# First 512 tokens as one block, blocks of 384 and 512 in turn, and the second batch's masks on VectorE

## The chip, the cores and the metric

The kernel runs on one core of one Trainium2 chip. The core has a matrix engine (TensorE, PE in the rows; PEld are its weight loads), a vector engine (VectorE, DVE), a scalar engine for activation functions (ScalarE, ACT), GpSimd (POOL) and SyncE (SP), which here issues all DMAs. The metric is the device time of one execution in microseconds.

## The reference, cut to what matters

Attention over 4 batches, 8 heads, 576 tokens and 64 dimensions a head; heads 0 to 3 see the 32 tokens before them (local), heads 4 to 7 see the tokens at a distance that is a multiple of 32 (strided). Its result goes through two feed-forward layers of 2304 tokens, width 512 and inner width 2048:

```python
scores = scale * q @ k.T                       # per batch and head
scores = where(mask_local or mask_strided, scores, -1e9)
x = softmax(scores) @ v                        # -> 2304 x 512
h = x @ moe_w_in ;  g = h * tanh(softplus(h)) ;  x = g @ moe_w_out
h = x @ moe2_w_in ; g = h - tanh(h)            ; y = g @ moe2_w_out
```

## The kernel before, in words

All products are done as three fp32r matmuls on high and low parts (high by high, low by high, high by low), which is why each weight and each activation is split into two parts.

**Attention** is done in half-pairs: a pair is two heads of one batch (`pair`, L492), each of its two halves 8 (strided) or 6 (local) score tiles. For a half PE computes the scores into two PSUM tiles `sps` (`score`, L577), VectorE takes the row maxima, ScalarE the exponentials `p`, PE transposes them (`ptps`, L697), they are copied to SBUF (`pT`), and PE multiplies with v (`ops`, L715). A batch in `LEAN` (L489) gets its mask from PE: before the scores, one bf16 matmul with the identity adds the mask to each of the two PSUM tiles (L586), VectorE then takes one maximum over a whole tile (`row_max`, L617), and the exponentials read PSUM. A batch that is not lean has no mask matmul; VectorE adds the mask and takes the maximum tile by tile in one instruction each (`masked_max`, L622) and writes the masked scores to SBUF. In a lean batch the division by the sum may be put on ScalarE (L665) or VectorE; in others it is VectorE's alone (L688). Batch 0 (`BY_PE`) has its sums made by PE (`tot`, L731).

**The first layer** goes over blocks of tokens, `blocks[0] = [256, 256, 512, 384, 512, 384]` (L262). A step is one block and one of 16 chunks c of the inner width (`step`, L841): 12 matmuls into `h` (L855), Mish on ScalarE into `B` (L874), the split of B into `gh` and `gl`, and two steps later (`LAG`) 12 matmuls into the four accumulators `acc` (L906). The moving operand is as wide as the block, so a matmul has 256, 384 or 512 columns. The first two blocks share the weights' arrival: five steps of block 0 run first, then block 1 and block 0 take turns (L349 to L351), and both write halves of the same accumulators. In batch 0, the second halves of the two local pairs (`LATE`, L462) have late due times, since block 0 needs only the first 256 tokens.

**The weights** of the first layer come by DMA as pairs of 32-bit words and are made into fp32 on VectorE (L414, L419, L424, three passes of 512 columns) and split (`wi`, `wo`, L449 to L455), while the first two blocks run. The second layer (`unit`, L1228) goes over its own blocks and is not touched, but for which spare buffers hold its parts of x.

**The order of all work** is set by `Plan.run` (L131): it lists tasks with due times and costs, and writes each engine's instructions in the order in which its own calculation has them start. Where it has PE idle for over 0.12 us before 196.6 us (`FILL`), it puts small filler matmuls there (`fill`, L475 to L479), at most the first part of the program. Batch b's attention is spread over the time before the block that needs it (L373 to L378); block data for the later blocks are stored to HBM and loaded again (`x_load`, L811), then split into `xh` and `xl` (`x_split`, L793).

Of the kernel before, what the change touches and what calls it, by code (L numbers as in the profile page):

```python
# [217 lines left out]
def pe_cost(n):  # L218
    return {256: 0.12, 384: 0.174, 512: 0.227}.get(n, 0.0004375 * n + 0.007)
# [23 lines left out]
def attention_two_moe(  # L243
# [15 lines left out]
    NC = 16  # L259
    WIN = 32  # L260
    scale = 1.0 / float(D) ** 0.5
    blocks = [[256, 256, 512, 384, 512, 384], [512] * 4 + [256]]  # L262
    TB = (512, 384)
    LAG = 2

# [9 lines left out]
    }  # L275
    starts = [[sum(bl[:j]) for j in range(len(bl))] for bl in blocks]

    pieces2 = [(0, starts[0][2])] + list(zip(starts[0], blocks[0]))[2:]
    x2d = {
        (p, i): dram.tile([128, n], F32, name=f"x2d{p}_{i}")  # L280
        for p in range(KC)
# [64 lines left out]
    add = plan.add  # L346


    steps = [(0, 0, c) for c in range(HEAD)]  # L349
    for c in range(NC):  # L350
        steps += [(0, 1, c)] + ([(0, 0, c + HEAD)] if c + HEAD < NC else [])  # L351
    steps += [(0, j, c) for j in range(2, len(blocks[0])) for c in range(NC)]
    NU, HALF = NC // 2, 256
    steps += [(1, j, u) for j in range(len(blocks[1])) for u in range(NU)]
    step_of = {x: s for s, x in enumerate(steps)}
# [2 lines left out]
    for l, j, c in steps:  # L358
        if l == 0 and j == 0:
            t_ = max(t_, FIRST + PACE * c)  # L360
        due.append(t_)
        if l == 0:
            t_ += 24 * pe_cost(blocks[l][j]) + (ATTEND if 1 < j < 5 else 0.0)
        else:
            t_ += (42 if blocks[1][j] > HALF else 24) * pe_cost(HALF) + 6 * blocks[1][j] // 128 * pe_cost(DM)
    due += [t_, t_ + 4, t_ + 8, t_ + 12]
    first_use = [min(step_of[0, j, c] for j in range(2)) for c in range(NC)]


    def block_of(token):  # L370
# [2 lines left out]
    x_due = [FIRST] + [due[step_of[0, block_of(S * b), 0]] - XLEAD for b in range(1, B)]  # L373
    ATT = {}
    for b in range(1, B):
        since = max(x_due[b - 1], due[step_of[0, 1, 0]])
        gap = (x_due[b] - since) / KC
        ATT[b] = (x_due[b] - KC * gap, gap)  # L378

# [79 lines left out]


    pairs = [(b, p) for b in range(B) for p in (2, 3, 0, 1)]
    LATE = (2, 3)  # L462
    pass
    AT = ["at0", "at1"]
    EARLY = ["h0", "h1", "acc0", "acc1", "acc2", "acc3"]

# [19 lines left out]
    last_s, last_load = {}, {}  # L486


    BY_PE, LEAN = (0,), (0, 1)  # L489
    ON_ACT = [(0, 0), (0, 1), (1, 0), (1, 1)]  # L490

    def pair(i):  # L492
# [272 lines left out]

        last_pv = []

        inner = starts[0][2]
        x_slot = ["xr0", "wi9", "wo9", "wi8"][i] if first else "xr0"
        xb = Buf([x_slot], 5) if first else Buf([x_slot], 1)  # L770
        done = [half_pair(0), half_pair(1)]
        plan.link(*done)
        cols = slice(inner, S) if first else slice(0, S)
        if first:
            for j in range(2):
                t0, n = starts[0][j], blocks[0][j]
                x_split(0, j, p, [done[0]] if i in LATE and j == 0 else done,
                        lambda t0=t0, n=n: st["x"][:, t0:t0 + n], xb,
                        k0 + 3 if j == 0 else due[step_of[0, 1, 0]] - 3)
            free_first[x_slot] = [split[j][p][1] for j in range(2)]  # L780
            for n, what in enumerate("qkv"):
                free_first[slot_of_first(i, what)] = last_s[i] if what != "v" else last_pv
        x_store[p, b] = add({SP: 0.45}, lambda e: nc.sync.dma_start(out=xd[p, b][:, cols], in_=st["x"][:, cols]),
                            k0 + 4, done, give=[xb], dma=0.3 if first else 0.9)
# [26 lines left out]
    def x_load(l, j, p, key):  # L811
        n, t0 = blocks[l][j], starts[l][j]
        if l == 0:
            pieces = [(b, b * S, b * S + S) for b in range(B)]
        else:
            pieces = [(i, s, s + m) for i, (s, m) in enumerate(pieces2)]
        cut = []
        for i, a, e in pieces:
            lo, hi = max(a, t0), min(e, t0 + n)
            if lo < hi:  # L820
                cut.append((i, lo, hi, a))
        buf = Buf(TMP, 2)
# [8 lines left out]
        after = [x_store[p, c[0]] if l == 0 else x2_store[p, 0, c[0] + 1] for c in cut]  # L831
        J = len(blocks[0]) * l + j
        x = add({SP: 0.45 * len(cut)}, load, key - 5, after + [last_g1[J - 2]], take=[buf], dma=0.7)
        x_split(l, j, p, [x], lambda: h["t"], buf, key)


# [4 lines left out]
    def step(s):  # L841
# [48 lines left out]
        B_done[s] = lo  # L890

        m = KC

        both = J < 2
        wide = starts[0][2] if both else n
        cols = slice(starts[0][J], starts[0][J] + n) if both else slice(0, wide)
        opens, closes = c == 0 and J != 1, c == NC - 1 and J != 0
        k2 = due[s + LAG] + 0.1
        for f in range(m):
            def gemm2(e, f=f):  # L900
                w = wts[l, "o", c]
# [14 lines left out]
            if closes:  # L916
                eb = Buf(TMP, 1)

                def evac(e, f=f, eb=eb):
                    t_ev[J, f] = t = sb([128, wide], F32, eb.slot, "ev")  # L920
                    if e == ACT:
                        nc.scalar.activation(out=t, in_=acc[f], func=ACTF.Copy, scale=2.0 ** -8)
                    else:
                        nc.vector.tensor_single_scalar(out=t, in_=acc[f], scalar=2.0 ** -8, op=ALU.mult)

                def store(e, f=f):
                    nc.sync.dma_start(out=x2d[f, j - 1], in_=t_ev[J, f])
# [192 lines left out]
    def factors(j, key, ready):  # L1120
# [5 lines left out]
        def load_of(x):  # L1126

            lower, half = x
            a0 = t0 + HALF * half
            cut = []  # L1130
            for i, (a, m) in enumerate(pieces2):
                lo, hi = max(a, a0), min(a + m, a0 + HALF)
                if lo < hi:
                    cut.append((i, lo, hi, a))
            buf = Buf(TMP, 2 if x == X22 else 1)

            def load(e):
# [5 lines left out]
            after = [x2_store[2 * lower + k, 0, i[0] + 1] for k in range(2) for i in cut] + old  # L1143
            return add({SP: 0.9 * len(cut)}, load, key - 5 + len(raw_loads), after, take=[buf], dma=0.7), buf

        def tiles():
# [9 lines left out]
            if J % 2 == 0:  # L1156
                lo = [hi.pop()] + [one_(sb([128, 2, HALF], F32R, slot, "xq")) for slot in ("q0", "q1", "k0", "k1")]
                t = sb([128, 4, HALF], F32R, "v", "xq")
                lo += [one_(t[:, :2]), one_(t[:, 2:])]
            else:  # L1160
                hi += [one_(sb([128, 2, HALF], F32R, "xr0", "xq"))]
                t = sb([128, 9, HALF], F32R, "pp", "xq")
                lo = [one_(t[:, 2 * i:2 * i + 2]) for i in range(4)]
                lo += [one_(cols(W2[u, 3][:, 1, :])) for u in (2 * NS, 2 * NS + 1)]
                lo += [two_(*(sb([128, 1, HALF], F32R, f"pT{i}", "xq") for i in range(2)))]
            xq[J] = list(zip(hi, lo))
            return xq[J]

# [246 lines left out]
    with tc.manual_schedule():  # L1415
# [8 lines left out]
        for c in range(NC):  # L1424
            for half in "io":
# [10 lines left out]
        for s in range(2 * NC):  # L1436
            step(s)
        last = len(blocks[0]) - 1
        for J in range(2, last + 1):
            if J < 2 + B - 1:  # L1440
                for i in range(KC * (J - 1), KC * J):
                    pair(i)
            for p in range(KC):
                x_load(0, J, p, due[NC * J] - XSPLIT + 0.7 * p)
# [33 lines left out]
        x, y = LATE  # L1478
        order[2 * x:2 * x + 4] = [(x, 0), (y, 0), (x, 1), (y, 1)]
# [57 lines left out]
```

## Time and profile before

| | |
|---|---|
| median of 3 runs | 892.72 us (891.67 to 892.78) |
| profiled execution | 891.31 us, span of the instructions 889.5 us |
| PE busy | 882.3 us (99% of the span) |
| VectorE busy | 593.0 us (67%) |
| ScalarE busy | 429.3 us (48%) |
| granted TensorE clock | 0.999 |

A row of the timeline is: start in us, length in us, engine, line, operation, out<-in, partitions by columns, count; a bracket at the end is idle time before it and what ended it. Matmul ends are modelled, so the spacing of starts is the better measure of what one costs. A program's time is some 1.8 us over its span.

### The profile page before, as it was taken

What the parts mean: (1) busy time and instruction counts of PE and PEld (TensorE: products, weight loads), DVE (VectorE), ACT (ScalarE), POOL (GpSimd) and SP (SyncE); (2) the same over time, 40 slices, a digit from 0 to 9 for tenths busy, and PEclk for the clock granted to TensorE, in tenths of its full rate; (3) what the DMA queues carried; (4) which work ended last, traced back from release to release, by engine and by line L of the source; (5) the groups of instructions that cost most, each with busy time, mean ns of one, the idle gap of its engine ahead of it and who ended that gap; (6) DMA issues with size and microseconds to landing.
All of it is one profiled execution on the core that took longest, in us unless ns stands there. A gap on an engine that the chain in (4) does not pass through costs nothing.

```text
span 889.5 us, 16480 instructions
## 1 busy us (share of the span) xinstructions
PE 882.3 (99%) x6080; PEld 788.3 (89%) x6080; DVE 593.0 (67%) x1578; ACT 429.3 (48%) x910; POOL 2.4 (0%) x13
## 2 busy tenths in 40 slices
PE   8999999999999999999999999999999999999998
PEld 7899999877778999888999999898999889998896
DVE  6999998556565657778776885575457545555533
ACT  7999999656446625443444532252224222322211
POOL 1000000000000000000000000000000000000000
PEclk9999999999999999999999999999999999999999
DMA  9981113411112149877787443352235223655531
GB/s 308 379 340 55 59 59 102 150 62 33 63 66 91 43 149 317 253 260 258 252 282 233 133 152 102 112 190 95 96 132 176 95 96 119 209 169 162 175 125 62
DMA packets 84657, 138.19 MB, mean 155 GB/s; under 512 B 10016, under 2 KB 37152, under 8 KB 84576
## 3 DMA queue, kind: packets, MB, share of 16 engines
q1 hardware_dynamic: 84576, 137.14, 46.1%
q8 instruction: 48, 0.79, 0.4%
q14 instruction: 33, 0.27, 0.1%
HBM read 107.22 MB, written 29.88 MB: 154 GB/s over the span
## 4 chain that ended last, share of the span: by engine, by line
PE 93%; ACT 4%; DVE 1%; DMA 1%; issue 0%; SPq 0%; ACTq 0%
PE acc L1382 22%; PE h L855 22%; PE acc L906 22%; PE hx L1245 18%; PE hx L1262 3%; PE sps L589 2%; PE ops L715 2%; PE ptps L697 2%; ACT p L645 1%; DMA kT<-in_k_dram 1%; ACT stwo L402 0%; ACT pT L449 0%; ACT L193 0%; ACT stwi L402 0%; ACT dd L735 0%
## 5 line engine op out<-in xcount | busy, mean ns | idle before, releaser
L855 PE MATMUL h<-xh,wi 128*128 128x256 f32 (+2 forms) x768 | 215.1, 342 | 0.6 <-ACT B L874 0.5
L906 PE MATMUL acc<-gh,wo 128*128 128x256 f32 (+2 forms) x768 | 196.5, 341 | 0.0
L1382 PE MATMUL acc<-w,gh 128*128 128x512 f32 x576 | 179.1, 392 | 0.0
L1245 PE MATMUL hx<-xq,w 128*128 128x256 f32 x1280 | 174.1, 284 | 0.0
L1245 PEld LDWEIGHTS hx<-xq,w 128*128 128x128 f32 x1280 | 167.6, 191 | 6.5
L855 PEld LDWEIGHTS h<-xh,wi 128*128 128x128 f32 x768 | 137.9, 189 | 14.4 <-ACT B L874 1.0
L906 PEld LDWEIGHTS acc<-gh,wo 128*128 128x128 f32 x768 | 132.1, 189 | 10.4
L855 PE MATMUL h<-xl,wi 128*128 128x256 f32 (+2 forms) x384 | 129.4, 337 | 0.1
L906 PE MATMUL acc<-gl,wo 128*128 128x256 f32 (+2 forms) x384 | 128.9, 336 | 0.0
L1382 PEld LDWEIGHTS acc<-w,gh 128*128 128x128 f32 x576 | 103.2, 188 | 18.1 <-DVE gh L451 0.4
L1382 PE MATMUL acc<-w,gl 128*128 128x512 f32 x288 | 112.2, 389 | 0.0
L1333 ACT ACTIVATE th<-hx 128x256 f32<-128x256 f32 x48 | 18.5, 385 | 160.2 <-PE hx L1245 120.1
L193 ACT ACT_TABLE_LOAD x70 | 89.8, 1283 | 1.2
L874 ACT ACTIVATE B<-h 128x256 f32<-128x256 f32 (+2 forms) x96 | 46.9, 492 | 89.5 <-PE h L855 87.0
L1338 DVE SCALAR_TENSOR_TENSOR H<-hx,th 128x256 f32<-128x256 f32 x48 | 20.3, 423 | 98.7 <-ACT th L1333 98.6
L455 DVE TENSOR_TENSOR gl<-B,gh 128x256 fp32r<-128x256 f32 (+2 forms) x96 | 52.9, 553 | 46.6 <-ACT gh L449 44.1
L1333 ACT ACTIVATE th<-H 128x256 f32<-128x256 f32 x64 | 33.5, 524 | 95.2 <-PE acc L1382 51.0
L455 DVE TENSOR_TENSOR H<-H,hx 128x256 f32<-128x256 f32 x160 | 66.9, 418 | 17.3 <-PE hx L1245 8.4
L906 PEld LDWEIGHTS acc<-gl,wo 128*128 128x128 f32 x384 | 72.5, 189 | 5.1
L855 PEld LDWEIGHTS h<-xl,wi 128*128 128x128 f32 x384 | 72.5, 189 | 5.0 <-DVE xl L455 0.3
L1382 PEld LDWEIGHTS acc<-w,gl 128*128 128x128 f32 x288 | 54.1, 188 | 12.1 <-DVE gl L455 0.2
L1338 DVE SCALAR_TENSOR_TENSOR H<-H,th 128x256 f32<-128x256 f32 x64 | 35.7, 558 | 40.2 <-ACT th L1333 39.9
(118 smaller groups left out, 1020.7 us busy)
## 6 DMA issues: line engine op xcount, KB each, us to landing
w<-w2o SPq DMA_DIRECT2D x160, 256.0 KB, 2.6
stwi<-in_moe_w_in_dram SPq DMA_DIRECT2D x16, 512.0 KB, 7.7
stwo<-in_moe_w_out_dram SPq DMA_DIRECT2D x16, 512.0 KB, 8.9
w2v<-in_moe_w_out_dram SPq DMA_DIRECT2D x32, 256.0 KB, 4.0
w2o<-p SPq DMA_DIRECT2D x48, 128.0 KB, 3.4
w<-w2i SPq DMA_DIRECT2D x24, 256.0 KB, 3.0
out_dram<-ev SPq DMA_DIRECT2D x18, 256.0 KB, 3.7
w2v<-in_moe_w_in_dram SPq DMA_DIRECT2D x8, 512.0 KB, 3.9
```

The source lines that it names most:

```text
L193: self.load_table(t.table)
L455: eng.tensor_tensor(out=out, in0=a, in1=b, op=op)
L589: nc.tensor.matmul(s[a][:, at_, :], tq[64 * a:64 * a + 64, q0:q0 + nq], tk[64 * a:64 * a + 64, k0_:k0_ + nk], start=not lean, stop=not lea ...
L697: nc.tensor.transpose(t[:, n, :], h["p", a][:, n, :], ident[:nq, :nq])
L855: nc.tensor.matmul(h_ps[s], w[:, wp, kc, :], xx[:, kc, :n], start=(kc == first_kc and i == 0), stop=(kc == last_kc and i == 2),)
L874: nc.scalar.activation(out=b_tile(), in_=h_ps[s], func=ACTF.Mish, scale=2.0 ** -8)
L906: nc.tensor.matmul(acc[f][:, cols], w[:, wp, 128 * f:128 * f + 128], g, start=(opens and i == 0), stop=(closes and i == 2),)
L1245: nc.tensor.matmul(st[t], w[:, wp, 256 * i + 128 * k:256 * i + 128 * k + 128], unit_of(xq[J][x][xp], k)[:, 0], start=(q in (1, 6, 7, 5) an ...
L1262: nc.tensor.matmul(st[t], w[:, wp], unit_of(xq[J][kc // 2][xp], kc % 2)[:, 0], start=(kc == 0 and m == 0), stop=(kc == KC - 1 and m == 2),)
L1333: nc.scalar.activation(out=st["th", i][:, cols], in_=x, func=ACTF.Tanh, scale=2.0 ** -8)
L1338: nc.vector.scalar_tensor_tensor(out=st["H", i][:, cols], in0=x, scalar=2.0 ** -8, in1=st["th", i][:, cols], op0=ALU.mult, op1=ALU.subtract,)
L1382: nc.tensor.matmul(acc[f], g[:, 128 * f:128 * f + 128], where[wp](), start=(opens and m == 0), stop=(closes and m == 2),)
```

## The change

Blocks of the first layer become `[512, 384, 512, 384, 512]`, so there are 80 steps in place of 96, each chunk of the first 512 tokens is done once with 512 columns, and the first step needs 512 tokens of batch 0. `LATE` is empty. `LEAN` is `(0,)`: batch 1 loses its mask matmuls and goes through `masked_max` and the other branches that batches 2 and 3 use. The rest adapts counts and buffers to five blocks (the blocks' alternating buffers swap roles for the second layer).

```diff
-    blocks = [[256, 256, 512, 384, 512, 384], [512] * 4 + [256]]
+    blocks = [[512, 384, 512, 384, 512], [512] * 4 + [256]]
...
-    steps = [(0, 0, c) for c in range(HEAD)]
-    for c in range(NC):
-        steps += [(0, 1, c)] + ([(0, 0, c + HEAD)] if c + HEAD < NC else [])
-    steps += [(0, j, c) for j in range(2, len(blocks[0])) for c in range(NC)]
+    steps = [(0, j, c) for j in range(len(blocks[0])) for c in range(NC)]
...
-    LATE = (2, 3)
-    pass
+    LATE = ()
...
-    BY_PE, LEAN = (0,), (0, 1)
+    BY_PE, LEAN = (0,), (0,)
...
-        inner = starts[0][2]
+        inner = starts[0][1]
...
-            for j in range(2):
-                t0, n = starts[0][j], blocks[0][j]
-                x_split(0, j, p, [done[0]] if i in LATE and j == 0 else done,
...
+            n = blocks[0][0]
+            x_split(0, 0, p, done, lambda: st["x"][:, :n], xb, k0 + 3)
...
-        both = J < 2
-        wide = starts[0][2] if both else n
-        cols = slice(starts[0][J], starts[0][J] + n) if both else slice(0, wide)
-        opens, closes = c == 0 and J != 1, c == NC - 1 and J != 0
+        wide, cols = n, slice(0, n)
+        opens, closes = c == 0, c == NC - 1
...
-        for J in range(2, last + 1):
-            if J < 2 + B - 1:
-                for i in range(KC * (J - 1), KC * J):
+        for J in range(1, last + 1):
+            if J < B:
+                for i in range(KC * J, KC * J + KC):
                     pair(i)
```

How the change moves instructions, at three places. First PE where the first layer begins; h is the first step's product, tot and ops are the last steps of a half-pair of batch 0, sps the scores of a half, and the rows left out in between are filler matmuls. The kernel before:

```order
L715 MATMUL ops<-pT,vl 64x96 x6
...
L855 MATMUL h<-xh,wi_475 128x256
L855 MATMUL h<-xl,wi_475 128x256
L855 MATMUL h<-xh,wi_475 128x256
...
L586 LDWEIGHTS identb
L586 MATMUL sps<-mfirst,identb 96x384
L589 MATMUL sps<-kT,qT 96x128 x6
L855 MATMUL h<-xh,wi_475 128x256
```

and the changed kernel:

```order
L848 MATMUL h<-xh,wi_469 128x512
L848 MATMUL h<-xl,wi_469 128x512
L848 MATMUL h<-xh,wi_469 128x512
L727 MATMUL tot<-pT,ones 64x288 x2
L711 MATMUL ops<-pT,vl 64x96 x6
...
L585 MATMUL sps<-kT,qT 72x72 x8
...
L848 MATMUL h<-xh,wi_469 128x512
L848 MATMUL h<-xl,wi_469 128x512
L848 MATMUL h<-xh,wi_469 128x512 x2
L848 MATMUL h<-xl,wi_469 128x512
L848 MATMUL h<-xh,wi_469 128x512
L693 MATMUL ptps<-ident,p 72x72 x8
```

Before, two half-pairs of batch 0 still have their scores behind the first three matmuls of h (six halves are complete there). Now all eight are complete ahead of the fourth matmul of h, and scores of two halves of batch 1 (sps without a mask row) stand ahead of it as well. Behind its first 57 filler matmuls the list before has 119 more, the changed one 98; in both none stands behind the third step.

Second, PE around the scores of a strided half-pair of batch 1, before:

```order
L855 MATMUL h<-xh,wi_1152 128x256
L586 LDWEIGHTS identb
L586 MATMUL sps<-mstrb,identb 72x288
L586 LDWEIGHTS identb
L586 MATMUL sps<-mstrb,identb 72x288
L589 MATMUL sps<-kT,qT 72x72 x8
L855 MATMUL h<-xh,wi_1152 128x256
```

and now:

```order
L848 MATMUL h<-xl,wi_798 128x512
L848 MATMUL h<-xh,wi_798 128x512
L585 MATMUL sps<-kT,qT 72x72 x8
L848 MATMUL h<-xh,wi_798 128x512
L848 MATMUL h<-xl,wi_798 128x512
```

The two mask matmuls and their weight loads are gone.

Third, VectorE at the maxima of such a half, before (L414 and L419 are passes over a weight):

```order
L455 TENSOR_TENSOR xl<-xr,xh 128x256
L617 TENSOR_REDUCE rows<-sps 72x4 x2
L638 TENSOR_SCALAR rows<-rows 72x4
L414 TENSOR_SCALAR wcv<-stwo_752 128x512
L638 TENSOR_SCALAR rows<-rows 72x4
L414 TENSOR_SCALAR wcv<-stwi_782 128x512
```

and now (of the eight pairs of ISA rows two are shown):

```order
L452 TENSOR_TENSOR xl<-xr,xh 128x512
L618 ISA p,rows<-sps,mstr 72x72
L618 ISA rows 72x1
L618 ISA p,rows<-sps,mstr 72x72
L618 ISA rows 72x1
...
L634 TENSOR_SCALAR rows<-rows 72x4
L452 TENSOR_TENSOR wi_798<-wcv,wi_798 128x512
L745 TENSOR_TENSOR xr<-ops,dd 128x288
```

The two maxima became eight masked maxima, each with the read of its result; the first such half stands between batch 0's third and fourth `xl`, that is ahead of the last input of the first step.

## Rows read from the trace of the kernel before

**Rows 1.** Page, the chain that ended last, by engine.

```profile
PE 93%; ACT 4%; DVE 1%; DMA 1%; issue 0%; SPq 0%; ACTq 0%
```

**Rows 2.** Waits of PE: us in total, times, longest.

```profile
PE h L855 <- ACT B L874: 0.5, 1, 0.5
```

**Rows 3.** Windows: length, busy PE, PEld, DVE, ACT, POOL, granted clock, DMA.

```profile
5.62:37.67 32.05, 30.21 (x439) 25.07 (x436) 29.48 (x74) 29.74 (x95) 0.00 (x0) 1.00 1.05 363
37.67:156.59 118.92, 118.35 (x1164) 110.27 (x1165) 113.24 (x350) 116.17 (x283) 0.00 (x0) 1.00 0.39 137
156.59:264.00 107.41, 107.41 (x712) 84.92 (x710) 61.96 (x256) 59.06 (x85) 0.00 (x0) 1.00 0.23 77
```

**Rows 4.** Timeline of PE, undisturbed steps of 256 and of 512 columns.

```profile
128.59 0.28 PE L855 MATMUL h<-xh,wi 128*128 128x256 f32 x1
131.47 0.28 PE L855 MATMUL h<-xh,wi 128*128 128x256 f32 x1
...
382.51 0.62 PE L906 MATMUL acc<-gh,wo 128*128 128x512 f32 x2
387.95 0.39 PE L906 MATMUL acc<-gh,wo 128*128 128x512 f32 x1
```

**Rows 5.** Timeline of PE, scores with masks (strided, local), then without (strided).

```profile
52.80 0.41 PE L586 MATMUL sps<-mstrb,identb 72*72 72x288 bf16 x2
53.14 0.74 PE L589 MATMUL sps<-kT,qT 64*72 64x72 f32 x16
...
125.44 0.49 PE L586 MATMUL sps<-mfirst,identb 96*96 96x384 bf16 x2
125.86 0.90 PE L589 MATMUL sps<-kT,qT 64*96 64x128 f32 x12
126.69 0.39 PE L855 MATMUL h<-xh,wi 128*128 128x256 f32 x1
...
133.26 0.28 PE L855 MATMUL h<-xh,wi 128*128 128x256 f32 x1
133.47 0.74 PE L589 MATMUL sps<-kT,qT 64*72 64x72 f32 x16
```

**Rows 6.** Timeline of PE: a transpose, the last fillers, tot with ops.

```profile
35.97 0.47 PE L697 MATMUL ptps<-ident,p 96*128 96x96 f32 x3
36.27 1.34 PE L479 MATMUL fill<-ones 128*128 128x128 bf16 x21
37.67 0.39 PE L855 MATMUL h<-xh,wi 128*128 128x256 f32 x1
...
48.69 0.71 PE L731 MATMUL tot<-pT,ones 128*64 128x288 f32 x4
49.82 0.39 PE L906 MATMUL acc<-gh,wo 128*128 128x256 f32 x1
```

**Rows 7.** Timeline of DVE: fourth xl, maxima, masked maxima (strided, then local).

```profile
32.43 0.41 DVE L455 TENSOR_TENSOR xl<-xr,xh 128x256 fp32r<-128x256 f32 x1
54.63 0.81 DVE L617 TENSOR_REDUCE rows<-sps 72x4 f32<-72x288 f32 x2
55.36 0.16 DVE L638 TENSOR_SCALAR rows<-rows 72x4 f32<-72x4 f32 x1
...
134.25 0.23 DVE L622 CUSTOM_DVE_ANT_0 p<-sps,mstr 72x72 f32<-72x72 f32 x1 [0.42 <-PE sps L589]
135.47 0.45 DVE L455 TENSOR_TENSOR p<-p,rows 72x288 f32<-72x288 f32 x1
135.84 0.45 DVE L451 COPY pT<-ptps 128x288 f32<-128x288 f32 x1
...
175.63 0.28 DVE L622 CUSTOM_DVE_ANT_0 p<-sps,mloc 96x128 f32<-96x128 f32 x1
176.89 1.02 DVE L455 TENSOR_TENSOR p<-p,rows 96x384 f32<-96x384 f32 x2
```

**Rows 8.** Groups by line and form, ACT: the division in batch 1.

```profile
L665 ACT ACTIVATE p<-p,rows 96x128 f32<-96x128 f32 x12 | 3.8, 398 | 0.0
```

More of the change, by code (lines that the diff above doesn't have):

```diff
@@ L276, in attention_two_moe @@
     starts = [[sum(bl[:j]) for j in range(len(bl))] for bl in blocks]
-    pieces2 = [(0, starts[0][2])] + list(zip(starts[0], blocks[0]))[2:]
+    pieces2 = list(zip(starts[0], blocks[0]))
     x2d = {
@@ L362, in attention_two_moe @@
         if l == 0:
-            t_ += 24 * pe_cost(blocks[l][j]) + (ATTEND if 1 < j < 5 else 0.0)
+            t_ += 24 * pe_cost(blocks[l][j]) + (ATTEND if j < 4 else 0.0)
         else:
@@ L366, in attention_two_moe @@
     due += [t_, t_ + 4, t_ + 8, t_ + 12]
-    first_use = [min(step_of[0, j, c] for j in range(2)) for c in range(NC)]
+    first_use = [step_of[0, 0, c] for c in range(NC)]
     def block_of(token):
@@ L375, in attention_two_moe @@
     for b in range(1, B):
-        since = max(x_due[b - 1], due[step_of[0, 1, 0]])
+        since = max(x_due[b - 1], due[step_of[0, 0, 1]])
         gap = (x_due[b] - since) / KC
@@ L766, in pair @@
         last_pv = []
-        inner = starts[0][2]
+        inner = starts[0][1]
         x_slot = ["xr0", "wi9", "wo9", "wi8"][i] if first else "xr0"
-        xb = Buf([x_slot], 5) if first else Buf([x_slot], 1)
+        xb = Buf([x_slot], 3) if first else Buf([x_slot], 1)
         done = [half_pair(0), half_pair(1)]
@@ L774, in pair @@
         if first:
-            for j in range(2):
-                t0, n = starts[0][j], blocks[0][j]
-                x_split(0, j, p, [done[0]] if i in LATE and j == 0 else done,
[L778 to L781, printed above, removed]
+            n = blocks[0][0]
+            x_split(0, 0, p, done, lambda: st["x"][:, :n], xb, k0 + 3)
+            free_first[x_slot] = [split[0][p][1]]
+            for n_, what in enumerate("qkv"):
                 free_first[slot_of_first(i, what)] = last_s[i] if what != "v" else last_pv
@@ L829, in load @@
                 nc.sync.dma_start(out=t[:, lo - t0:hi - t0], in_=src[:, lo - a:hi - a])
-        after = [x_store[p, c[0]] if l == 0 else x2_store[p, 0, c[0] + 1] for c in cut]
+        after = [x_store[p, c[0]] if l == 0 else x2_store[p, 0, c[0]] for c in cut]
         J = len(blocks[0]) * l + j
-        x = add({SP: 0.45 * len(cut)}, load, key - 5, after + [last_g1[J - 2]], take=[buf], dma=0.7)
+        x = add({SP: 0.45 * len(cut)}, load, key - 5, after + [last_g1.get(J - 2)], take=[buf], dma=0.7)
         x_split(l, j, p, [x], lambda: h["t"], buf, key)
@@ L926, in store @@
                 def store(e, f=f):
-                    nc.sync.dma_start(out=x2d[f, j - 1], in_=t_ev[J, f])
+                    nc.sync.dma_start(out=x2d[f, j], in_=t_ev[J, f])
                 ev = add({ACT: act_cost(wide, True), DVE: dve_cost(wide)}, evac, k2 - 8, [x], take=[eb], give=[ab])
@@ L1141, in load @@
                         nc.sync.dma_start(out=t[:, k, lo - a0:hi - a0], in_=x2d[2 * lower + k, i][:, lo - a:hi - a])
-            after = [x2_store[2 * lower + k, 0, i[0] + 1] for k in range(2) for i in cut] + old
+            after = [x2_store[2 * lower + k, 0, i[0]] for k in range(2) for i in cut] + old
             return add({SP: 0.9 * len(cut)}, load, key - 5 + len(raw_loads), after, take=[buf], dma=0.7), buf
@@ L1155, in tiles @@
             hi = [one_(t[:, 2 * i:2 * i + 2]) for t in (a, b) for i in range(m)]
-            if J % 2 == 0:
-                lo = [hi.pop()] + [one_(sb([128, 2, HALF], F32R, slot, "xq")) for slot in ("q0", "q1", "k0", "k1")]
+            if J % 2 == 1:
+                lo = [one_(sb([128, 2, HALF], F32R, slot, "xq")) for slot in ("q0", "q1", "k0", "k1", "xr0")]
                 t = sb([128, 4, HALF], F32R, "v", "xq")
                 lo += [one_(t[:, :2]), one_(t[:, 2:])]
+                hi += [two_(*(sb([128, 1, HALF], F32R, f"pT{i}", "xq") for i in range(2)))]
             else:
-                hi += [one_(sb([128, 2, HALF], F32R, "xr0", "xq"))]
+                lo = [hi.pop()]
                 t = sb([128, 9, HALF], F32R, "pp", "xq")
-                lo = [one_(t[:, 2 * i:2 * i + 2]) for i in range(4)]
+                lo += [one_(t[:, 2 * i:2 * i + 2]) for i in range(4)]
                 lo += [one_(cols(W2[u, 3][:, 1, :])) for u in (2 * NS, 2 * NS + 1)]
-                lo += [two_(*(sb([128, 1, HALF], F32R, f"pT{i}", "xq") for i in range(2)))]
             xq[J] = list(zip(hi, lo))
@@ L1435, in attention_two_moe @@
                 weights(0, half, c, free_first.get(tag, []), due_w - 3.514, kd)
-        for s in range(2 * NC):
+        for s in range(NC):
             step(s)
         last = len(blocks[0]) - 1
-        for J in range(2, last + 1):
-            if J < 2 + B - 1:
-                for i in range(KC * (J - 1), KC * J):
+        for J in range(1, last + 1):
+            if J < B:
+                for i in range(KC * J, KC * J + KC):
                     pair(i)
```

2 lines of the change are left out of this document (removed).

## The prediction

> **What bounds the kernel now.** I read the chain of work that ended last, then PE's waits, then the windows of the first stages, then PE's timeline for the spacing of matmuls. The chain is PE for 93% of the span [rows 1]; ScalarE's 4% lie almost all in the first 38 us, where attention of batch 0 is made. From 37.67 us on PE is hardly ever idle: 118.35 of 118.92 us until the second 512 tokens' block begins at 156.59 us, and all of the next 107.41 us [rows 3]. The one wait there is 0.5 us for ScalarE [rows 2]. The granted clock is 1.00 throughout, the 2.4 GHz level [rows 3]. So after 37.67 us the time is the sum of PE's instructions, and before it, it is how soon VectorE and ScalarE deliver batch 0. VectorE is nearly full as long as the weights are made: 113.24 of 118.92 us, then 61.96 of 107.41 us [rows 3]. That is the engine to which the change gives work.
>
> **Part 1: 768 matmuls of 256 columns become 384 of 512.** 24 undisturbed matmuls of 256 columns take 131.47 - 128.59 = 2.88 us, 120.0 ns each; 24 of 512 take 387.95 - 382.51 = 5.44 us, 226.7 ns each [rows 4]. Two narrow ones cost 240.0 ns, one wide one 226.7: 13.3 ns saved, 384 times, 5.1 us. All of it is on the path, since PE is the chain there.
>
> The same rows give a slope of 106.7 ns for 256 columns and a fixed 13.3 ns for each matmul [rows 4]. The Trainium skill (TensorE: Matmul & The Clock Gate, section Back-to-back issue gap) states a fixed part of about 2.5 ns, by which this term would be 1.0 us and the time about 886.9 us. Another page of the Trainium skill (TensorEngine Tiling (Array Packing), section Instruction Overhead) states about 60 cycles a matmul, an estimate of 25 ns, by which it would be 9.6 us and the time 878.3. The trace lies between the two, and the measurement decides.
>
> **Part 2: batch 1 without mask matmuls.** Eight half-pairs, four strided and four local. A strided half's two masks take 53.14 - 52.80 = 0.34 us, a local one's 125.86 - 125.44 = 0.42 [rows 5]. What remains is not quite as short: where scores come without a mask, PE has about 0.09 us between the end of the preceding matmul (133.26 + 0.12) and their start at 133.47 [rows 5], and the mask hides that gap. So 0.25 and 0.33 us a half: 4 x 0.25 + 4 x 0.33 = 2.3 us, on the path.
>
> **Part 3: the start.** The first step now needs 512 tokens, so all eight half-pairs of batch 0. I compare the point where PE's gap-free run begins: before, 37.67 us, with two halves of batch 0 still to finish; now, the fourth kc of the first step. Ahead of that point PE's list now holds, more than before: one score set with masks, 126.69 - 125.44 = 1.25 us; two scores of batch 1 without, 0.76 each, 1.5; four transposes at about 0.28, 1.1 (one takes up to 36.27 - 35.97 = 0.30); tot and ops of two halves, 49.82 - 48.69 = 1.13 each, 2.3; nine matmuls of 512, 2.0; less 24 of 256, 2.9 [rows 4 to 6]. Together 5.3 us. Had fillers and waits stayed as they are, the run would begin at 43.0 us, and each microsecond earlier is a gain.
>
> The upper bound for the new point: 98 fillers in place of 119 behind the first 57, at 1.40/21 = 0.067 us [rows 6], with the other waits as before: 43.0 - 1.4 = 41.6 us. The lower one is from VectorE, which makes the last `xl` that the run waits for. Before, the fourth `xl` ends at about 32.43 + 0.34 [rows 7]. Now two more halves of batch 0 stand ahead of it (two maxima of 384 columns at about 0.47, two small ones and a multiplication of about 0.45: 1.5 each, 3.1), four `xl` are 256 columns wider (about 0.27 each, 1.1), and the first half of batch 1 (8 masked maxima in 135.47 - 134.25 = 1.22 us, reciprocals 0.6, a division 0.37 [rows 7]: 2.2). That is 6.4 us later, 39.2 us. I take 40 us, nearer to VectorE's, since it releases the last input: 3.0 us gained. Both ends are kept: 1.4 to 3.8.
>
> **Part 4: VectorE's and ScalarE's added work.** A strided half's maxima take 1.22 us where they took 55.36 - 54.63 = 0.73; a local half's 176.89 - 175.63 = 1.26 where two maxima of 384 columns take about 0.94 [rows 7]. 4 x 0.49 + 4 x 0.32 = 3.2 us more. The division of four local tiles that ScalarE had (12 instructions [rows 8]) goes to VectorE, 4 x 0.47 = 1.9, with two strided tiles 0.7 more. The wider `gl` saves about 32 x 0.335 - 16 x 0.60 = 1.1. Net about 4.7 us more on VectorE, which PE covers as long as VectorE keeps ahead. The window: from 40 us to 156.6 - 10.4 = 146.2, 106 us, for 113.2 + 4.7 us less the 2.2 that now come before 40 us: 115.7. That does not fit as a whole, but before, VectorE did four strided halves of batch 2 within this window, at about 4.2 us each (masked maxima 1.22, sums 0.73, reciprocals 0.6, divisions 0.74, copies 0.9), and in the new order three of them stand ahead of the last `gl` of the block. And the last results are due some 6 us after the next block's start, as the second product of a step runs two steps later. So 111.5 us of work against 106 + 6: covered, with little to spare. The rest of batch 2 falls into the next block, where VectorE has 45 us free [rows 3]. I charge 1.0 us for short waits in place of the 0.5 us of before, 0.5 net. At full price, with each overrun waited for, it is 5 us.
>
> Removed late loads and the swapped buffer roles cost nothing that I can find: the loads of batch 0 are 0.9 MB moved earlier, while the weights of the first steps are done by VectorE later than they arrive; the last four blocks have their inputs split a whole block ahead.
>
> **Sum.** 5.1 + 2.3 + 3.0 - 0.5 = 9.9 us, from the profiled execution's 891.3 to 881.4. The median of the runs is 1.4 us above that execution: 882.8 us.
>
> **Rivals.** (a) VectorE paces the first block. Then PE waits for `gl` or a weight again and again between 60 and 150 us. For it: VectorE at 95% there [rows 3], and each masked maximum waits in VectorE's queue for scores, with weight passes behind it (0.42 us idle ahead of the first one [rows 7]). Against it: the three halves of batch 2 are the only work that could be late without harm, and they come last. Price 3 to 6 us: 886 to 889. (b) On the other side, slower: VectorE's queue is in order. If all four halves of batch 2 stand ahead of the block's last results, VectorE is idle for the 5.7 us of before [rows 3], and each of batch 1's eight halves adds 0.42 us of waiting for scores [rows 7], 3.4, the last results come at 40 + 115.7 + 5.7 + 3.4 = 164.8 us. Less the 6 us by which they are due later, the next block starts at 158.8, where 156.6 was: 2.2 us slower, 894.9. It decides once PE's waits in the first block exceed 10.4 us; below that the change still gains. (c) The start gains nothing or loses: the eight halves are done late, for instance because ScalarE, also full until then (29.74 of 32.05 us [rows 3]), holds two more halves at about 3 us each before the first step and the run begins at 46 us. Then the third term is -3 and the time 888.8. (d) The clock falls in the start. Up to the scores of batch 0's last half the new list has 4 fillers behind the first 57; the granted clock never fell in the kernel before [rows 3]. If PE's pauses brought it to 1.2 GHz and the first two steps ran there, 48 matmuls of 512 would cost 0.227 us more each, 10.9 us: 893.7, slower by a hair or no change.
>
> The Trainium skill (TensorE: Matmul & The Clock Gate, section HAM oscillation — how this bites in real kernels) warns that a long enough wait between bursts of matmuls takes the clock back down. In the trace here the pauses of the start did not: the granted clock is 1.00 in that window.
>
> **How the numbers follow.** Forecast (880 to 886) 0.69; more than 12.5 us gained, by a start at 39 us and no waits, 0.04; (a) 0.13; (c) 0.06; (d) 0.03; (b) 0.05. What a measurement of this kernel can tell from no change is about 0.2%, 1.8 us, so faster means below 890.9. The forecast, the larger gain, (c) and most of (a) are faster: 0.89. Within 0.2%: a worse (a), half of (d): 0.05. Slower: (b) and the other half of (d): 0.06. The range 880 to 888.5 leaves out (b), (d), the end of (a) and of (c), and the largest gains.
>
> **What would show it.** Right: the same spacing of 227 ns for the 512-column matmuls of the first 16 steps; PE's gap-free run from 39 to 42 us; no mask rows in batch 1; idle of PE after that point of at most 2 us; the block after the first 512 tokens starting some 10 to 13 us before 156.6 (partly because less of batch 2 stands ahead of it). Wrong: PE waiting for VectorE (`gl`, `wi`, `wo` or the split x) by several microseconds between 60 and 150 us, a granted clock below 1.00, or a wait of PE at the starts of the later blocks, where batch 2 now has a 384-column block to finish in.

## The result, and the profile after

The changed kernel takes 882.89 us (median of 4 runs, 882.27 to 883.53), the kernel before took 892.56 beside it. The ratio is 0.988, with a 95% interval from 0.9842 to 0.9919; by the medians it is 9.7 us or 1.1% faster. The prediction was 882.8 us. The sum came out, but three of its four terms did not, and the traces and experiments show which.

The profiled execution of the changed kernel took 882.96 us (span 881.2), that of before 891.3 (span 889.5); the spans differ by 8.3 us, since the profiled run of before was 1.25 us below its median. All that follows on traces is about these 8.3 us.

The chain that ended last, by engine, answers to [rows 1]:

```profile
PE 96%; ACT 2%; DMA 1%; issue 0%; SPq 0%; DVE 0%
```

PE's waits answer to [rows 2] (total, times, longest). Each of these is over by 34.4 us; the wait for `B` is gone.

```profile
PE ptps L693 <- ACT dd L731: 1.8, 5, 0.5
PE fill L475 <- DVE ones L1409: 1.0, 1, 1.0
PE sps L585 <- DMA kT<-in_k_dram: 0.9, 1, 0.9
PE tot L727 <- ACT pT L446: 0.2, 1, 0.2
```

The windows answer to [rows 3]. The second block of the first layer now begins at 145.27 us, where it began at 156.59:

```profile
5.62:38.00 32.38, 29.40 (x434) 23.10 (x431) 28.99 (x91) 28.90 (x102) 0.00 (x0) 1.00 1.05 353
38.00:145.27 107.27, 107.26 (x746) 83.82 (x742) 105.54 (x369) 100.73 (x235) 0.00 (x0) 1.00 0.43 151
145.27:264.00 118.73, 118.73 (x884) 105.21 (x883) 74.62 (x319) 74.56 (x108) 0.00 (x0) 1.00 0.27 86
```

PE is busy for 107.26 of 107.27 us. VectorE has 1.7 us idle in the same stretch. ScalarE, which was the fuller of the two helpers before (116.17 of 118.92 us [rows 3]), now has 6.5 us.

A stretch of PE's timeline in the first block answers to [rows 4]. Twelve matmuls of 512 columns take 104.05 - 101.33 = 2.72 us, 226.7 ns each:

```profile
101.33 0.39 PE L848 MATMUL h<-xh,wi 128*128 128x512 f32 x1
...
104.05 0.61 PE L896 MATMUL acc<-gh,wo 128*128 128x512 f32 x2
```

Where the time came from can be read from PE's timeline by adding up the distance from each instruction's start to the next one's, by kind (idle time apart, without the first 1.0 us; sums worked out from all rows of both traces):

| kind | before us | after us | difference |
|---|---|---|---|
| first layer's matmuls (h, acc) | 414.7 | 409.7 | -5.1 |
| mask matmuls | 6.3 | 3.2 | -3.2 |
| scores | 24.1 | 24.2 | +0.1 |
| fillers | 11.8 | 10.9 | -0.9 |
| idle, up to 38 us | 1.6 | 2.9 | +1.2 |
| idle, later | 0.5 | 0.0 | -0.5 |
| transposes, ops, tot | 40.8 | 41.2 | +0.4 |
| second layer, and what follows PE's last matmul | 388.6 | 388.2 | -0.4 |

So the traces give 5.1 us for the width, 3.0 for the masks and 0.5 for a wait that is gone. The start, which is fillers and the idle time up to 38 us, has lost 0.3. That number is no finer than one execution allows: with the same list up to there, the changed kernel and runs 3, 4 and 8 below have their first matmul of h at 35.52, 35.53, 34.45 and 34.85 us.

The start itself, in PE's timeline:

```profile
35.52 0.50 PE L848 MATMUL h<-xh,wi 128*128 128x512 f32 x1
...
37.55 1.74 PE L475 MATMUL fill<-ones 128*128 128x128 bf16 x28
39.22 0.74 PE L585 MATMUL sps<-kT,qT 64*72 64x72 f32 x16
39.89 1.29 PE L475 MATMUL fill<-ones 128*128 128x128 bf16 x20
40.99 0.48 PE L848 MATMUL h<-xh,wi 128*128 128x512 f32 x1
...
42.48 0.67 PE L693 MATMUL ptps<-ident,p 72*72 72x72 f32 x8
42.95 0.48 PE L848 MATMUL h<-xh,wi 128*128 128x512 f32 x1
```

PE goes on at 40.99 us with the second kc, and the fourth starts at 42.95. I had it at 40. VectorE's last `xl`, which answers to [rows 7], and ScalarE's last `xh` ahead of it:

```profile
39.38 0.34 ACT L641 ACTIVATE p<-p,rows 72x72 f32<-72x72 f32 x1
39.72 0.62 ACT L446 ACTIVATE xh<-xr 128x512 fp32r<-128x512 f32 x1
...
40.37 0.69 DVE L452 TENSOR_TENSOR xl<-xr,xh 128x512 fp32r<-128x512 f32 x1
```

That `xl` is over at 40.98 us, when VectorE's next instruction starts, and PE goes on at 40.99, as its twenty fillers end. It is the second kc's, not the fourth's, since the kernel takes the pairs of a batch in the order 2, 3, 0, 1 (`pairs`). Six matmuls and eight transposes, which I had put ahead of that moment, come behind it.

One thing changed that I had not looked at. ScalarE's table loads, from 38 us to the start of the block after the first 512 tokens, in the groups by line (count, busy us, mean ns, idle before), of before and of the changed kernel:

```profile
L193 ACT ACT_TABLE_LOAD x36 | 46.2, 1283 | 0.6
```

```profile
L193 ACT ACT_TABLE_LOAD x22 | 28.2, 1283 | 0.4
```

The Trainium skill (ScalarE: Activation LUTs, section What ACT_TABLE_LOAD costs) gives 1283 ns for a load too, and a drain of about 1380 ns on top. In the trace here the load of 1.28 us is the whole price: ScalarE goes on with the next activation as it ends, and no drain shows.

```profile
44.23 0.19 ACT L641 ACTIVATION_READ_ACCUMULATOR p<-p,rows 72x1 f32 x1
44.44 1.28 ACT L193 ACT_TABLE_LOAD   x1
45.73 0.60 ACT L867 ACTIVATE B<-h 128x512 f32<-128x512 f32 x1
```

ScalarE changes its table between the activation of a step (Mish) and attention's exponentials. With 16 steps in place of 32 there are 14 loads fewer in the stretch, 18.0 us of ScalarE. By the counts, the planner gave ScalarE copies and casts that VectorE had done. VectorE's groups of before in that stretch:

```profile
L451 DVE CAST gh<-B 128x256 fp32r<-128x256 f32 x14 | 3.9, 283 | 0.0
L451 DVE COPY xr<-ops 128x288 f32<-128x288 f32 x6 | 3.7, 620 | 0.3 <-PE ops L715 0.2
L451 DVE CAST wo<-wcv 128x512 fp32r<-128x512 f32 x7 | 2.9, 407 | 0.0
```

and the same three in the changed kernel, 10.5 us down to 3.6:

```profile
L448 DVE CAST gh<-B 128x512 fp32r<-128x512 f32 x4 | 1.7, 416 | 0.0
L448 DVE COPY xr<-ops 128x288 f32<-128x288 f32 x2 | 1.5, 731 | 0.0
L448 DVE CAST wo<-wcv 128x512 fp32r<-128x512 f32 x1 | 0.4, 392 | 0.0
```

### The profile page after: what moved, and what is told of

Same layout as the page of the kernel before. It is cut to its first block, busy times and chain, and to the rows that moved or that the text cites. A ratio compares the mean times of both kernels' runs of the same rounds, so it can differ in the third digit from the quotient of the medians.

```text
span 881.2 us, 15610 instructions
## 1 busy us (share of the span) xinstructions
PE 873.5 (99%) x5659; PEld 762.5 (87%) x5659; DVE 587.4 (67%) x1629; ACT 418.4 (47%) x875; POOL 2.4 (0%) x13
## 4 chain that ended last, share of the span: by engine, by line
PE 96%; ACT 2%; DMA 1%; issue 0%; SPq 0%; DVE 0%
PE h L848 23%; PE acc L896 23%; PE acc L1372 22%; PE hx L1235 19%; PE hx L1252 3%; PE sps L585 2%; PE ops L711 2%; PE ptps L693 2%; ACT p L641 1%; DMA kT<-in_k_dram 1%; PE fill L475 1%; ACT pT L446 0%; ACT dd L731 0%; ACT dd L734 0%; PE tot L727 0%
## 5 line engine op out<-in xcount | busy, mean ns | idle before, releaser
L848 PE MATMUL h<-xh,wi 128*128 128x512 f32 (+1 forms) x640 | 206.2, 376 | 0.0
L896 PE MATMUL acc<-gh,wo 128*128 128x512 f32 (+1 forms) x640 | 187.0, 373 | 0.0
L848 PEld LDWEIGHTS h<-xh,wi 128*128 128x128 f32 x640 | 118.9, 188 | 17.8 <-ACT B L867 0.2
L896 PEld LDWEIGHTS acc<-gh,wo 128*128 128x128 f32 x640 | 115.7, 188 | 14.2
L848 PE MATMUL h<-xl,wi 128*128 128x512 f32 (+1 forms) x320 | 118.0, 369 | 0.0
L896 PE MATMUL acc<-gl,wo 128*128 128x512 f32 (+1 forms) x320 | 117.9, 368 | 0.0
L867 ACT ACTIVATE B<-h 128x512 f32<-128x512 f32 (+1 forms) x80 | 44.4, 555 | 84.8 <-PE h L848 84.5
L452 DVE TENSOR_TENSOR gl<-B,gh 128x512 fp32r<-128x512 f32 (+1 forms) x80 | 50.9, 636 | 46.9 <-ACT gh L446 44.5
L193 ACT ACT_TABLE_LOAD x58 | 74.4, 1283 | 1.0
L896 PEld LDWEIGHTS acc<-gl,wo 128*128 128x128 f32 x320 | 60.1, 188 | 7.8
L848 PEld LDWEIGHTS h<-xl,wi 128*128 128x128 f32 x320 | 60.2, 188 | 6.5
```

The source lines that it names most:

```text
L193: self.load_table(t.table)
L452: eng.tensor_tensor(out=out, in0=a, in1=b, op=op)
L848: nc.tensor.matmul(h_ps[s], w[:, wp, kc, :], xx[:, kc, :n], start=(kc == first_kc and i == 0), stop=(kc == last_kc and i == 2),)
L867: nc.scalar.activation(out=b_tile(), in_=h_ps[s], func=ACTF.Mish, scale=2.0 ** -8)
L896: nc.tensor.matmul(acc[f][:, cols], w[:, wp, 128 * f:128 * f + 128], g, start=(opens and i == 0), stop=(closes and i == 2),)
```

## The experiments

The theory to start with was that of the prediction: from about 41 us on TensorE's list sets the time, the parts add, and VectorE covers its share. The main rival was (a), VectorE pacing the first block. Times are medians; the kernel before was timed beside each group (892.21 us with the first four, 892.01 with the second, 892.03 with the third). The changed kernel was not timed again with them. The kernel before took 892.56 us beside it, 0.35 to 0.55 more than in the groups, so a distance to the changed kernel is uncertain by about half a microsecond. In runs 1, 2 and 5 to 8 the planner also makes a new order of the whole work; runs 3, 4, 9 and 10 keep the changed kernel's.

**1. The widths alone.** Batch 1's masks go back to TensorE:

```
-    BY_PE, LEAN = (0,), (0,)
+    BY_PE, LEAN = (0,), (0, 1)
```

> The changed kernel, with batch 1's masks added by TensorE again: the widths of the blocks alone are changed against the kernel before. Theory (from about 41 us on TensorE's list of instructions sets the time): the mask matmuls and the longer scores come back, 3.16 - 0.14 = 3.0 us by the two traces, so 885.9 us; by the 2.3 us of the prediction 885.2. Rival (VectorE paces the first block, so that moving the masks to it bought nothing): 883 or below.

Measured: 887.91 us, ratio 0.997 (0.9935 to 1.0004), 5.0 us above the changed kernel. So the masks are worth more than I had, not less, once the blocks are wide. Of the 4.9 us between the two spans PE's timeline gives 3.0 to the mask matmuls and 1.0 to fillers; the other 0.9 is spread over the second layer, and I have no cause for it. The widths alone are worth 892.21 - 887.91 = 4.3 us.

**2. The masks alone.** The kernel before, with its narrow blocks and late halves, and

```
-    BY_PE, LEAN = (0,), (0, 1)
+    BY_PE, LEAN = (0,), (0,)
```

> The kernel before, with batch 1's masks added by VectorE: the mask part alone, on the narrow blocks. Theory (the parts add): 892.6 - 3.0 = 889.6 us (2.3 by the prediction's size: 890.3). Rival (with blocks of 256 the waits of TensorE for batch 1's attention and for VectorE grow by what is removed, since each block leaves less time for the same attention work): 892 to 894.

Measured: 894.59 us, ratio 1.0023 (1.0007 to 1.004): 2.4 us slower than before. The rival, whose range ended at 894, was nearer, and the theory that the parts add has fallen: -4.3 and +2.4 make -1.9, and together they give -9.7. PE's waits and the one wait in its timeline show where, and so do three groups of fillers in the middle of the block, where before had none (49 fillers, 2.9 us in all, put there since the planner's own calculation has PE idle):

```profile
PE h L855 <- ACT B L874: 1.4, 1, 1.4
```

```profile
63.99 0.39 PE L855 MATMUL h<-xh,wi 128*128 128x256 f32 x1 [1.41 <-ACT B L874]
...
86.62 1.46 PE L479 MATMUL fill<-ones 128*128 128x128 bf16 x23
...
110.65 0.95 PE L479 MATMUL fill<-ones 128*128 128x128 bf16 x14
...
112.48 0.83 PE L479 MATMUL fill<-ones 128*128 128x128 bf16 x12
```

The window from 38 to 158.5 us has both helpers full: VectorE 117.90 of 120.50 us, ScalarE 116.58, with 38 table loads.

```profile
38.00:158.50 120.50, 118.64 (x1207) 111.17 (x1207) 117.90 (x453) 116.58 (x267) 0.00 (x0) 1.00 0.41 142
```

**3. Part 1 by itself.** The changed kernel in its own order, but every matmul of the first block issued as two halves:

```
+                for t0, t1 in ((0, 256), (256, 512)) if J == 0 else ((0, n),):
-                nc.tensor.matmul(h_ps[s], w[:, wp, kc, :], xx[:, kc, :n], ...)
+                    nc.tensor.matmul(h_ps[s][:, t0:t1], w[:, wp, kc, :], xx[:, kc, t0:t1], ...)
```

and the same for `acc`.

> The changed kernel, its order kept, but each of the 384 matmuls of the first block issued as two of 256 columns. Part 1 as forecast (13.3 ns for each matmul more): + 5.1 us, 888.0. If a matmul costs only 2.5 ns beside its columns: + 1.0, 883.9. If the 18.9 ns that the two traces show for a pair in the first layer, attention's insertions included, is the matmuls' own: + 7.3, 890.2.

Measured: 886.37 us, ratio 0.9932 (0.9907 to 0.9957), 3.5 us above the changed kernel, 9.1 ns for each of the 384 matmuls. In an undisturbed step the price is the forecast one: 24 halves take 103.15 - 100.27 = 2.88 us, 240.0 ns a pair against 226.7.

```profile
100.27 0.64 PE L899 MATMUL acc<-gh,wo 128*128 128x256 f32 x4
...
103.15 0.40 PE L849 MATMUL h<-xh,wi 128*128 128x256 f32 x2
```

Over the whole first block h and acc take 97.3 us against 94.1. At the undisturbed spacing they would take 92.2 and 87.1, so what lies around the insertions of attention is 5.1 us with halves and 7.1 with whole matmuls. The 5.1 us of Part 1 are paid, and about 2 come back beside attention. Narrow matmuls do not lose less there in every order: the kernel before needs 99.0 us for its 768, 6.8 more than the undisturbed spacing. Why the halves of this run lose less was not tried.

**4. VectorE loaded further.** In the first block gl is subtracted twice:

```
             sub(e, gl_t[s], B_t[s], gh_t[s].bitcast(F32))
+            if J == 0:
+                sub(e, gl_t[s], B_t[s], gh_t[s].bitcast(F32))
```

> The changed kernel with one more subtraction of 128x512 on VectorE in each of the 16 steps of the first block (the same result written twice): 16 x 0.68 = 10.9 us more of VectorE between 48 and 147 us. Theory (VectorE's results lie 5.8 to 11.9 us ahead of their use by TensorE in steps 1 to 15, and 2 us of the stretch are idle): at most 3 us are seen, 882.9 to 885.9. Rival (VectorE, at 39.74 of 40 us busy, paces the first block): 8 to 11 us, 891 to 894.

Measured: 893.05 us, ratio 1.0011 (0.9984 to 1.0038), 10.2 us above the changed kernel: nearly all of the 10.9 us is seen (8.8 in the profiled execution, with a span of 890.0 us). I had argued with the 6 to 12 us by which gl lies ahead of its use. That slack isn't the one that counts: PE waits for the masked maxima, which share VectorE's queue with the added work.

```profile
PE ops L711 <- DVE rows L618: 5.5, 4, 2.3
PE ptps L693 <- DVE rows L618: 1.1, 2, 0.9
```

In TensorE's list, multiplications of attention stand among the steps at places that the planner chose for the time at which VectorE would be done. What is late there holds up everything behind it, with the next step's inputs long ready.

So VectorE has next to no room. Two questions were open: whether room is what the masks alone lacked, and whether VectorE already costs the changed kernel something.

**5 and 6. Room for the narrow blocks.** Both kernels read gh in place of gl in the first two blocks and leave its subtraction out, which takes a part out of the result:

```
-        lo = add(pairs_of(n), e9, ka + .8, [hi])
+        lo = hi if J < 2 else add(pairs_of(n), e9, ka + .8, [hi])
-                gh, gl = gh_t[s], gl_t[s]
+                gh, gl = gh_t[s], gh_t[s] if J < 2 else gl_t[s]
```

> The kernel before, without VectorE's 32 subtractions gl of the first two 256-blocks; the second product reads gh in their place, so TensorE's work is the same and a part of the result is left out. It takes 32 x 0.34 = 10.9 us from VectorE in the first 147 us. TensorE waits for nothing but 0.5 us there, so by every theory the time is that of before less 0 to 0.5 us: 891.7 to 892.2.

> The mask part alone on the narrow blocks, again without the 32 subtractions gl. Theory (the mask part lost 2.4 us there since VectorE had no room for it): with 10.9 us of room it gives what its matmuls cost, 3.0 us against the kernel before without gl, 889. Rival (a masked maximum costs in itself, by its longer way from the scores to the transposes, however much room VectorE has): 2 us over the kernel before without gl, 894.

Measured: 893.32 us (ratio 1.0016, 0.9998 to 1.0033) without the mask part and 891.45 (0.9999, 0.998 to 1.0018) with it. With room on VectorE the mask part gains 1.9 us on the narrow blocks, where without room it lost 2.4. The rival's 2 us over the kernel without gl is out, and the runs agree with room being what the part lacked. They do not show it alone, since each of the kernels has its own order. The first of the two is 1.3 us above before, though it has less to do, which is a miss: I had expected no more than 892.2. So an order by itself can be worth more than a microsecond, and no other order was tried for the mask part on narrow blocks. The gain of 1.9 is short of the 3.0 expected, and what holds the rest stays open (ScalarE keeps its 37 table loads there; the trace, of an execution 3.2 us above the median, has one wait of PE of 2.3 us for VectorE's `p`).

**7. Room for the changed kernel.** The same omission in the first block of the changed kernel (`J == 0` in place of `J < 2`).

> The changed kernel without VectorE's 16 subtractions gl of the first block (the second product reads gh in their place, a part of the result is left out): 10.9 us less on VectorE. Theory (VectorE is just covered: it doesn't set the time, though any addition shows): 882.4 to 883.1. Rival (VectorE paces the first block already, in pauses of TensorE too short to be shown as waits): 880 or less.

Measured: 882.71 us, ratio 0.9909 (0.9881 to 0.9936), 0.2 below the changed kernel, or 0.4 above it by the distances to the kernel before beside each. VectorE does not set its time: 10.9 us less of it change nothing that these runs can tell, 10.9 us more cost 10.2. It is covered, with next to no room.

**8. Attention of batch 1 later.** To see whether its first half, which stands among the last splits of the start, holds the start up:

```
-        since = max(x_due[b - 1], due[step_of[0, 0, 1]])
+        since = max(x_due[b - 1], due[step_of[0, 0, 3]])
```

> The changed kernel with attention of batch 1 due from the fourth step on, not from the second. Theory for the start (VectorE's and ScalarE's work on batch 1's first half stands ahead of the last split of the first block, so the fourth kc is 2 us late): the fourth kc starts at about 41 us, where it was 42.95, and the time is 881. Rival (the start is full of TensorE's own work, and what is moved out of it meets a full VectorE later): 883 to 885.

Measured: 884.78 us, ratio 0.9918 (0.9895 to 0.9941), 1.9 slower than the changed kernel. The last `xl` starts at 39.74 us, where it was 40.37, but in this execution the first matmul of h is 0.67 us earlier too (34.85 for 35.52): counted from there, the `xl` comes no sooner. It is over at 40.34, and PE runs on only from 40.78 us, behind 70 fillers in place of a score and 48; the fourth kc starts at 42.2, not at 41:

```profile
36.88 4.08 PE L475 MATMUL fill<-ones 128*128 128x128 bf16 x70
40.78 0.47 PE L848 MATMUL h<-xh,wi 128*128 128x512 f32 x1
```

The fillers in all are 22 more (177 where it was 155), and behind the first 57 they take 1.1 us more. The theory is wrong: without batch 1's first half the last split comes no sooner, so that half was using time that the start had anyway. The fillers are the larger part of the 1.9 us; the rest I did not trace.

**9 and 10. What ends the start.** The four `xl`, or the four `xh`, of the first block are made twice:

```
             sub(e, xl[J][:, p, :n], src(), xh[J][:, p, :n].bitcast(F32))
+            if J == 0:
+                sub(e, xl[J][:, p, :n], src(), xh[J][:, p, :n].bitcast(F32))
```

and `copy(e, xh[J][:, p, :n], src())` likewise.

> The changed kernel with the four subtractions xl of the first block made twice (the same result): 4 x 0.60 = 2.4 us more on VectorE ahead of the first step's last input. Theory (VectorE's list up to 41 us is full and sets when the start ends): 2 to 2.4 us more, 885. Rival (the start ends by ScalarE's last split or by TensorE's own work): at most 0.6 us more, 883.5.

> The changed kernel with the four copies xh of the first block made twice (the same result): 4 x 0.52 = 2.1 us more on ScalarE ahead of the first step's last input. If ScalarE's list sets the end of the start as well as VectorE's (exponentials of batch 1 stand right ahead of its last copy): about 2 us more, 885. If VectorE's list alone sets it: 0.5 us, the last copy's own part of the chain, 883.4.

Measured: 885.69 us (ratio 0.9922, 0.9897 to 0.9946) and 886.19 (0.9947, 0.9912 to 0.9981), 2.8 and 3.3 us above the changed kernel for 2.4 and 2.1 us of added work. All of what was added is seen on both engines, so both lists set the end of the start. Why run 10 loses more than was added stays open; the granted clock fell in its profiled execution, so its trace can't show it. With `xl` twice, PE waits for it where it did not before:

```profile
43.34 0.48 PE L850 MATMUL h<-xh,wi 128*128 128x512 f32 x1
44.21 0.50 PE L850 MATMUL h<-xl,wi 128*128 128x512 f32 x1 [0.38 <-DVE xl L452]
```

**11 and 12. Another order.** The planner's constants alone are changed, eight in one kernel (gathered here from their lines), four in the other:

```
-FIRST_PE, XSPLIT, FIRST, XLEAD = 25.0, 25.0, 24.0, 8.0
+FIRST_PE, XSPLIT, FIRST, XLEAD = 29.289, 22.914, 24.222, 14.492
-HOLD, HOLDW, HOLDO, LOADW = 28.118, 4.936, 1.818, 1.963
+HOLD, HOLDW, HOLDO, LOADW = 41.904, 1.693, 1.992, 2.677
```

> The changed kernel with other constants for the order of the work (eight of them: FIRST_PE 29.289, XSPLIT 22.914, FIRST 24.222, XLEAD 14.492, HOLD 41.904, HOLDW 1.693, HOLDO 1.992, LOADW 2.677), 129 fillers where it had 155. If the start is a matter of order: 26 fillers at 0.067 us less, 1.7 us, 881.2. Rival (VectorE and ScalarE are full up to 147 us, so another order only moves the waiting): 882.5 or more.

> The changed kernel with four other constants for the order (XSPLIT 27.517, HOLDW 1.48, AHEAD 3.073, LOADW 1.821). The same question as in the run with eight constants: 881.3 if the order alone can win back part of the start, 882.5 or more if it can't.

Measured: 881.50 us (881.23 to 881.64; ratio 0.9861, 0.9822 to 0.9901) and 881.76 (881.12 to 882.24; 0.9864, 0.9824 to 0.9904). The first is 1.4 us below the changed kernel, as expected, or 0.9 by the distances to the kernel before beside each, and against before the intervals of the two overlap. PE's run begins at 39.55 us, with fewer fillers ahead; not all of the 1.4 us between 39.55 and 40.99 is order, since in this execution kT did not keep PE waiting, where the changed kernel's trace has 0.9 us for it:

```profile
38.62 1.11 PE L475 MATMUL fill<-ones 128*128 128x128 bf16 x17
39.55 0.48 PE L848 MATMUL h<-xh,wi 128*128 128x512 f32 x1
```

This is the version to keep: the same work in a better order, with 26 fillers less.

## Why the prediction was right, and where it was not

*What bounds the kernel*: right. TensorE's list sets the time from 41 us on, before and after; run 7 shows that VectorE does not, within half a microsecond. What was to show it came: 226.7 ns a matmul, no idle time of PE after 34.4 us, and the second block 11.3 us sooner.

*Part 1, 5.1 us*: the traces give 5.1 for h and acc as they stand, the isolated run 3 gives 3.5. The price of 13.3 ns holds in undisturbed steps. I multiplied it by all 384 matmuls without asking what they lose beside attention's insertions. That loss is 6.8 us before and 7.1 after, so nearly the same, and the term came out; in run 3, with halves in the changed kernel's order, it is 5.1, and there the same width is worth less. By the fixed part of about 2.5 ns that the Trainium skill (TensorE: Matmul & The Clock Gate, section Back-to-back issue gap) states for an isolated matmul, the term would have been 1.0 us, an estimate. Run 3 measured 3.5 in all and 13.3 ns in clean stretches, so the trace stands against the small figure here.

*Part 2, 2.3 us*: mis-sized. The traces show 3.0, since the gap of 0.09 us that I charged to each score without a mask [rows 5], 0.7 in all, does not come back as time. The scores as a whole grew by 0.1 us, and h and acc, to which the gap ahead of a score counts in the table, take 409.6 us in run 1 with the masks and 409.7 in the changed kernel without. Beyond that the part as I costed it does not exist by itself. On the narrow blocks it loses 2.4 us (run 2), on the wide ones it is worth 5.0 (run 1).

*Part 3, 3.0 us*: the step that failed. The start lost 0.3 us. I forecast "the fourth kc of the first step" at 40 us, between 39.2 and 41.6, nearer to VectorE's bound, "since it releases the last input". It was 42.95, outside the bounds and level with the 43.0 that meant no gain. By what one execution differs from another the gain may be up to 1 us, not 3. Two things were wrong. The last `xl` came at 40.98, not at 39.2: ScalarE's exponentials of batch 1 stood ahead of the last `xh`, and PE's first wait for kT was 0.2 us longer (0.9 against 0.7). And that `xl` belongs to the second kc, so 2.0 us of TensorE's own work come behind it. Runs 9 and 10 show that both helpers set this point, where I had counted VectorE alone. It is rival (c) in its first half, "the start gains nothing". Order alone wins 0.9 to 1.4 us back (run 11).

*Part 4, 0.5 us charged*: the charge was not needed, no wait is left after 34.4 us, and the 0.5 us of before is gone. The verdict "covered, with little to spare" holds (runs 4 and 7). The working behind it had the wrong reason: I forecast 4.7 us more on VectorE, and its busy time over the span went from 593.0 to 587.4 us. The pages of runs 1 and 2 part the two:

```profile
PE 877.6 (99%) x5693; PEld 764.8 (86%) x5693; DVE 583.9 (66%) x1532; ACT 419.1 (47%) x894; POOL 2.4 (0%) x13
PE 883.3 (99%) x6113; PEld 789.9 (89%) x6113; DVE 597.5 (67%) x1679; ACT 428.9 (48%) x893; POOL 2.4 (0%) x13
```

With all that the planner then moves between the helpers, the masks alone bring VectorE 4.5 us more (597.5), or 3.5 beside the wide blocks (587.4 against 583.9), where I had 5.8. The widths alone take 9.1 us off it (583.9), where I had credited 1.1 for gl. The counts point to the reason: wide blocks freed 18 us of ScalarE's table loads in the first block, and ScalarE took copies and casts over; no run tries this by itself. Only three strided halves of batch 2 remain in the stretch (24 tiles of masked maxima, where it was 31 of before's four halves), as I had argued.

The total was right because errors cancel, which is luck. By the traces the four terms are 5.1, 3.0, -0.3 and +0.5, in sum 8.3 us, where I had 5.1, 2.3, 3.0 and -0.5, in sum 9.9. The 1.6 us too much were made up by the 1.4 that I added for the median, since the profiled execution of the changed kernel lies at its median (882.96 and 882.89). *Rival (a)* did not happen, but run 4 shows how near it was: 10.9 us more on VectorE bring it about.

*Rival (d)* did not happen in the profiled execution (granted clock 1.00 in all three windows above), but it was near. In run 7's profiled execution, 893.00 us where the median is 882.71, the granted clock was 0.50, the 1.2 GHz level, from 12 to 38 us, behind a wait of PE for kT of 1.46 us, where the changed kernel's trace has 0.89. The kernel before has it too, with 900.56 and 900.78 us at a mean clock of 0.986 in two of the 23 executions beside runs 9 to 12. Run 7's page gives the clock in tenths, by slices of 22 us:

```profile
PEclk7699999999999999999999999999999999999999
```

## What to carry to other kernels

Cost an edit's second-hand work too: half as many steps cut ScalarE's table loads in the first block from 36 to 22, and VectorE, with the widths alone, had 9.1 us less to do, of which I had foreseen 1.1. When a change has two parts, ask whether one pays for the other; here the masks cost 2.4 us alone and bring 5.0 beside the wide blocks. And an engine busy at 98% with no wait behind it may be covered and yet have no room: test it in both directions before giving it more, and look for its slack at the result that is due soonest, not at the one with the longest lead.

## What the runs showed of the hardware that was not expected

A masked maximum costs VectorE less than its own two instructions: eight tiles of 72x72 start 0.15 us apart, 0.22 us long each, with the read of the accumulator under the next one.

```profile
33.84 0.22 DVE L618 CUSTOM_DVE_ANT_0 p<-sps,mstr 72x72 f32<-72x72 f32 x1
34.00 0.22 DVE L618 CUSTOM_DVE_ANT_0 p<-sps,mstr 72x72 f32<-72x72 f32 x1
```

A table load takes 1283 ns of ScalarE each time; the whole span has 70 of them from L193 before, 58 after and 54 in the reordered kernel. And what the first layer's matmuls lose beside the insertions of attention is about as large as what their width is worth: 7.1 us over the first block with whole matmuls, 5.1 in the same order with halves, 6.8 in the kernel before.
